# Batch 4's q through the DMA crossbar as well, with a new order and three fewer filler matmuls

## The chip, the cores and the metric

The kernel runs on one core of a Trainium2 chip, one launch, all inputs in HBM. The time is the device time of one execution in microseconds (us); less is better. TensorE (PE) multiplies matrices and writes PSUM, VectorE (DVE) and ScalarE (ACT) work element by element and read PSUM, GpSimd (POOL) here makes a few small products and issues most loads, and SyncE (SP) issues DMA transfers. Each engine runs its instructions in the order in which they were issued.

## What is computed

An attention of the kind in which k and v are first multiplied, and then a gated channel mix on its output. Cut to what matters:

```python
# q, k, v: (8 batches, 8 heads, 576, 64)
q_s = softmax(q, axis=-1)              # over the 64 of a head
k_s = softmax(k, axis=2)               # over the 576 positions
kv  = einsum('bhsd,bhse->bhde', k_s, v)
x   = einsum('bhsd,bhde->bhse', q_s, kv)   # then heads side by side: (8, 576, 512)
x_prev = x shifted by one position
xk = mu_k * x + (1 - mu_k) * x_prev
xr = mu_r * x + (1 - mu_r) * x_prev
k  = relu(xk @ w_k)                    # 512 -> 1024
v  = (k * k) @ w_v                     # 1024 -> 512
out = sigmoid(xr @ w_r) * v
```

Inputs and output are float32; the products are made in bfloat16.

## The kernel before, in words

Batches are taken one after another, and of each batch two groups g of four heads: `b4g1` below is batch 4, group 1, and an operation's name carries both (`scale41`, `B41`). A group's q, k and v arrive in three loads of 576 KB each (`load41q0`, `load41k0`, `load41v0`), issued by POOL into 11 buffers; batches 0 and 1 are cut finer.

For one group: ACT takes exp of q and k (`expq`, `expk`, L345) and casts v (`cast`, L352); DVE sums q's rows (`rsum`, L360), inverts the sums (`rrec`, L364) and scales (`scale`, L369). The scaled q must be turned, so that the 64 of a head lie on partitions. This is done in one of two ways:

- For batches 2 to 4 TensorE turns it: 36 (or, in larger pieces, 18) transposes into PSUM (L386), and one ACT copy of PSUM into the buffer `qt` (`qt40`, L397).
- For the batches in `CROSS` the DMA turns it: one `dma_start_transpose` on SP's queue from `qs` to `qt` (`tq50`, L559), from SBUF to SBUF.

k and v are multiplied on TensorE (L419). DVE makes weights of the product (`rz`, `w`, L426 and L436). The product of the turned q with these weights (L576) is `x`. From batch 2 on the pieces are joined into blocks on TensorE: block `B41` first makes `x` of the group before it (b4g0), then turns its own q if TensorE does that, and then multiplies its own k and v. So `B41` waits for q of b4g0 to be turned. Behind it ACT copies `x` (`xb`, `xs`) and DVE makes the two mixes (`edge`, `diff`, `sc`, `mix`, L589 to L603). Batches 0 and 1 have smaller steps for the same work: `Z` (sums of k, L406), `KV`, `T` (turning q, L386), `rz`, `kvn`, `qt`, `wp` (weights, L509) and `X` (L520).

The channel mix runs over 4608 positions in 11 units of 256 to 512 columns: `k5_3` is unit 5, piece 3 of the 8 of w_k (L680), followed by `relu` on ACT (L659) and `sq` on DVE (L669). For each of 36 tiles of 128 positions there are `r17` (L713), `th17` (tanh on ACT, L718), `v17_0` and `v17_1` (L733), `o17` (DVE, L739) and two stores `st17` (L749) on SP's queue.

What sets the order is the string `ORDER`: one list of all operations of all engines by name. Each engine executes its own in the order of the list; PSUM banks and buffers stand behind the colon. `POOL!` before a name chooses an engine. `^name` behind a name is a hold: the operation also waits until the named one is done, for a load until it has landed.

```python
name, _, held = name.partition("^")
...
if op.held:
    tc.add_manual_dep(op.made.ins, op.held.made.ins.name, sync)
```

At the start, before data is there, TensorE multiplies zeros: 19 `fill` (512 columns, L302) and `GAPS` small ones, `fillgap` (256 columns, L311), whose places are in the list too. Their output is not used.

Of the kernel before, what the change touches and what calls it, by code (L numbers as in the profile page):

```python
# [56 lines left out]
X0000:0 edge01 wp010:1 ACT!x0001b load11k0:6 x0000a DVE!x0010 X0100:1 ACT!x0000b X0101:3 x0100a  # L57
X0011:0 ACT!x0101b load11v1:7 x0100b k0_0:0 x0101a k1_0:1 x0011 k0_0.2 POOL!wp011 k1_0.2 k1_3:2
relu1_0:0 k1_7:3 load11k1 k0_1 k0_2:1 relu0_0:1 X0110:1 k1_3.2 load10q1 sq0_0 k1_7.2 k1_5:0
relu1_7:2 k0_2.2 load11v0 expq111:2 X0111:0 sq1_7 DVE!x0110 k0_4:3 wv0 relu1_3:1 k1_5.2 k0_4.2  # L60
sq1_0 relu1_5:2 k1_4:2 load10v0:8 rsum111:2 k0_5 expq110 k1_6:0 k1_4.2 sq1_3 relu0_4:0 k1_6.2
sq1_5 rrec111 relu1_4:1 x0111 k0_6:3 k0_3 relu1_6:2 k1_1:2 expq100:1 sq0_4 k1_2:0 k0_6.2 rsum110
relu0_2:0 wv1 k1_2.2 k1_1.2 k0_7 sq0_2 load10v1 r1:1 rrec110 relu1_1:0 scale110:2 load10k0:9 r2:2
sq1_1 scale111 load10k1 relu1_2:0 th1:0 r0:0 cast111:0 expk111:2 wv2 sq1_6 rsum100:3 T11:1 expq101
cast110 r3:1 expk110 sq1_2 load20q0:10 rsum101 relu0_6:2 KV11 th0:1 rrec101 sq1_4 th3:2 rz11:2
kvn11:0 load20v0:0 v0_0:3 sq0_6 th2:3 DVE!wp111:0 ACT!cast100:1 load21q0:1 v1_0:0 qt111:2 rrec100
qt110 scale101:0 v3_0:1 load30q0:2 scale100 v1_1 wp110 cast101 v0_1 load20k0:3 expk100:0 T10:0
v3_1 DVE!qt100:1 expk101 qt101 X1101:1 KV10 edge10 ACT!x1101 edge11 rz10:0 v0_2 kvn10:1 v3_2
POOL!wp100:1 o0 v1_2 load21v0:4 X1001:1 expq200:0 o1 X1000:0 X1110:3 load21k0:5 x1001 st1 v2_0:0
x1000 load30k0:7 DVE!x1110 cast200:2 X1111:1 load31q0:6 rsum200:1 X1100:0 k2_1:2 load40q0:8 x1100  # L70
v2_1 k2_7:3 expq210:2 wp101 rrec200 o3 k2_1.2 v2_2 load61v0:9 relu2_1:0 k2_2:1 o2 k2_7.2 expq300:1
load50k0:10 k2_0:2 x1111 k2_2.2 relu2_7:1 sq2_1 k2_5:0 rsum300:0 load31k0:0 k2_0.2 expk200:1
k2_4:3 X1010:0 relu2_2:2 X1011:1 scale200:1 load40v0:1 k2_4.2 relu2_0:0 k2_3:1 x1010 k2_6:2 sq2_7
cast210:0 k2_3.2 sq2_0 load30v0:2 k2_5.2 x1011 k2_6.2 relu2_5:1 rsum210:2 TKV20:0 relu2_4:0
load40k0:3 expk210:2 r5:0 rz20:1 rrec300 rrec210 r7:3 w20:0 th5:4 sq2_5 load31v0:4 scale210:2
relu2_3:1 r6:0 qt20:0 r4:1 load41q0:5 scale300:0 th7:5 B21:1.0 expq310:0 sq2_2 sq2_4 r8:3 rz21:2
relu2_6:2 sq2_3 load41v0:6 rsum310:3 xs20:0 th4:6 v4_0:2 xb20 v6_0:1 sq2_6 w21:1 th6:7 rrec310
edge20 v4_1 diff20:0 qt21:2 v6_1 scale310:1 th8:8 X21:0.1 v5_0:0 xb21:1 sc2001:0 sc2000 v4_2 o6
xs21 expk300:0 v7_0:3 edge21 st6 mix200 v5_1 st0 cast300:1 diff21:1 load51q0:7 st3 v7_1 sc2101:1
st2.2 expk400:1 sc2100 load60q0:2 mix210 st0.2 TKV30:0 cast310:2 o7 st3.2 load41k0:3 k3_4:1 st2 o5  # L80
expq400:2 k3_0:3 load70v0:4 sc2011:2 rz30:0 sc2111:0 k3_6:0 w30:2 relu3_4:0 sc2110 load70q0:8
sc2010 relu3_0:1 o4 k3_1:1 expk310:2 mix201 k3_5:3 mix211 relu3_1:2 load61q0:0 k3_3:2 qt30:1 sq3_1
sq3_4 k3_2:1 sq3_0 relu3_3:2 rsum400:1 relu3_5:0 B31:1.0 relu3_2:1 rrec400 k3_7:2 sq3_3 xb30:0
sq3_2 sq3_5 v8_0:3 xs30 relu3_6:2 rz31:1 scale400:2 r9:1 relu3_7:1 expq410:1 v10_0:0 sq3_7 w31:0
edge30 th9:9 sq3_6 r10:2 load50q0:5 diff30:1 cast400:0 v9_0:1 sc3001:1 sc3000 qt31:0 load51v0:1
sc3011:2 v8_1 mix300 expk500:0 B40:0.1 rsum410:2 th10:1 v10_1 load71v0:10 rz40:2 o8 xb31:1 r11:2
o10 st8.2 xs31 expq700:0 st5 edge31 v11_0:3 diff31:0 st6.2 v9_1 th11:2 sc3100:0 load71q0:8 st5.2
sc3101 expq510:2 rrec410 st7 v11_1 sc3010 mix310 st4 expk410:2 r12:0 load61k0:7 scale410:0 st8
k4_6:2 th12:3 load70k0:3 o11 expq500:1 k5_6:0 o9 k4_7:3 rsum510:0 relu4_6:0 st9.2 load51k0:5
k4_3:1 relu4_7:1 st10 cast510:1 k5_4:2 st9 rrec510 sq4_7 k4_0:3 sc3110:1 relu4_3:2 sc3111  # L90
load50v0:1 sq4_6 k5_5 relu4_0:1 mix311 k5_2:1 relu5_4:0 k5_7 sq4_0 cast410:2 k4_2:3 sq5_4 w40:1
scale510:1 k4_5:2 relu4_2:1 load71k0:6 relu5_6:0 k4_1:3 mix301 expq600:2 sq4_3 k5_3 sq4_2 k4_4:0
relu4_1:2 sq5_6 load60k0:2 rsum500:3 relu4_5:1 k5_0:3 relu4_4:0 r14:2 qt40:2 rsum600:1 k5_1 r13:0
th14:7 sq4_1 cast500:0 rrec600 B41:1.0 rrec500 sq4_5 sq4_4 th13:4 load60v0:1 scale600:2 v13_0:2
xs40:1 relu5_0:2 r15:0 xb40 rz41:0 sq5_0 w41:2 v12_0:3 relu5_2:1 edge40 diff40:1 th15:8 v15_0:1
qt41:1 scale500:0 v13_1 expk510:1 sc4001:0 tq50:0 B50:0.1 o13 st10.2 cast600:2 v12_1 rsum700:2
v15_1 xb41:0 rz50:1 o12 r16:0 expk610:2 w50:0 st12 sq5_2 v14_0:2 sc4010:1 st13.2 sc4000 xs41 o15
expk710:0 st13 v16_0:3 edge41 st12.2 mix400 th16:9 r17:1 st7.2 sc4011 expq710:2 diff41:0 tq51:2
B51:1.0 sc4110:2 cast610:0 v16_1 rrec700 sc4101:0 sc4100 v17_0:0 mix410 expk600:1 rz51:2 o16 v14_1
th17:1 mix401 expq610:1 k6_4:3 o14 k6_0:1 v17_1 sc4111 xs50:1 st14 xb50 w51:1 mix411 st4.2 k6_1  # L100
k6_2:2 rsum610:0 st1.2 relu6_0:0 B60:1.0 st11.2 k6_3 tq60:1 xb51:0 sq6_0 k6_5 st15.2 rz60:0
rrec610 edge50 r19:1 o17 st11 relu6_4:2 diff50:1 xs51 st16 k6_6:0 th19:4 r18:3 edge51 diff51:0
expk700:1 k6_7 sc5101:0 r20:1 sc5000:1 th18:3 sc5100 relu6_2:1 sq6_4 r21:3 w60:2 relu6_6:0 sq6_2
sq6_6 v19_0:2 th21:5 sc5010:2 mix510 th20:6 v18_0:0 sc5001 mix500 v19_1 sc5011 B61:0.1 o19 k7_3:3
sc5110:0 mix501 k7_2:1 scale700:0 relu7_3:2 xb60:1 k7_0:2 scale610:1 relu7_2:1 k7_6:3 relu7_0:0
k7_1:1 sc5111 tq61:0 rz61:1 sq7_3 tq70:2 mix511 v18_1 relu7_6:2 st14.2 cast700:1 sq7_6 k7_4:2
sq7_2 rsum710:1 relu7_1:2 k7_5:3 relu7_4:1 r23:1 o18 sq7_1 k7_7:2 sq7_0 th23:0 w61:0 relu7_5:2
r25:0 xs60 relu7_7:0 edge60 sq7_4 B70:1.0 sq7_7 rrec710 v21_0:1 diff60:1 xs61:0 xb61 v22_0:3
sc6000:1 th25:2 edge61 diff61:0 v20_0:2 cast710:2 sc6001 r22:0 rz70:2 sc6110:2 sq7_5 w70:1 v21_1
# [12 lines left out]
th31:3 st27.2 o31 v30_0:0 relu10_6:2 relu10_5:0 st31.2 k10_1:2 st28 sq10_5 v30_1 st28.2 relu10_1:0
st22.2 sq10_1 r34:3 sq10_6 sq10_7 st31 v32_0:1 o30 th34:5 st17.2 r32:2 st30 st23 v32_1 th32:4
v35_0:3 o32 v33_0:0 st32.2 v34_0:2 st30.2 st32 r33:1 v33_1 th33:9 v34_1 o33 r35:1 st33.2 o34 st33
v35_1 th35:2 st34 v35_0.2:0 st34.2 o35 v35_1.2 st35.2 st35 o35.2 st35.4 st35.3
"""


# [770 lines left out]
```

## Time and profile before

| | us |
|---|---|
| median of 3 runs | 198.97 |
| lowest, highest | 198.77, 198.99 |
| the profiled execution's own time | 198.85 |
| its span, from the first to the last instruction | 196.9 |
| TensorE busy in the span | 188.0 (95%) |
| VectorE busy | 151.9 (77%) |
| ScalarE busy | 134.9 (69%) |
| GpSimd busy | 47.7 (24%) |

HBM is read for 33.56 MB and written for 9.44 MB; the mean granted TensorE clock is 0.98. The profile's page gives totals over the span; its views by stretch, by time and by engine, and the chain of work that ended last, give single instructions with their start and length in us. A matmul's length in these views includes its way through the array, so the time that it takes in a row of matmuls is read from one start to the next.

### The profile page before, as it was taken

The page shows a single profiled execution, that of the slowest core. Times are in us where ns is not written, and L with a number is a line of the kernel's source. Part 1 is how long each engine was busy: PE and PEld are TensorE (multiplying, and loading weights), DVE is VectorE, ACT ScalarE, POOL GpSimd, SP SyncE. Part 2 cuts the span into 40 slices and gives each one's busy share as a digit, 9 for nine tenths or more (in the row PEclk, how much of TensorE's full clock was granted, in tenths as well). Part 3 has the DMA queues.
Part 4 walks back from the last instruction along what each step waited for, and adds up shares of the span by engine and source line. Part 5 has one row for each costly group of instructions (what it writes and reads, how often), then busy time and mean ns, then how long its engine had stood idle before and what let it go on. Part 6 is the DMA issues. An engine that isn't in the chain of part 4 may idle for free.

```text
span 196.9 us, 4779 instructions
## 1 busy us (share of the span) xinstructions
PE 188.0 (95%) x1894; PEld 96.1 (49%) x1916; DVE 151.9 (77%) x343; ACT 134.9 (69%) x213; POOL 47.7 (24%) x79
## 2 busy tenths in 40 slices
...
GB/s 188 348 203 295 348 256 359 398 239 392 392 389 387 315 416 297 298 312 413 318 148 168 103 171 64 16 134 0 57 168 107 0 42 41 19 142 118 202 83 160
DMA packets 23702, 41.87 MB, mean 213 GB/s; under 512 B 9460, under 2 KB 12800, under 8 KB 23680
## 3 DMA queue, kind: packets, MB, share of 16 engines
...
q14 instruction: 7, 0.06, 0.1%
HBM read 33.56 MB, written 9.44 MB: 218 GB/s over the span
## 4 chain that ended last, share of the span: by engine, by line
PE 79%; DVE 9%; ACT 5%; DMA 2%; issue 2%; POOL 0%; DVEq 0%; POOLq 0%
PE mm_b L680 9%; PE mm_c L680 8%; PE mm_d L680 8%; PE mm_d L733 7%; PE mm_c L733 7%; PE mm_a L733 7%; PE mm_a L680 6%; PE mm_a L713 4%; PE mm_b L733 4%; PE mm_b L713 4%; PE mm_c L713 2%; DMA raw_a<-in_q_dram 2%; PE mm_d L713 2%; PE att_a L419 2%; PE att_b L419 1%
## 5 line engine op out<-in xcount | busy, mean ns | idle before, releaser
L733 PEld LDWEIGHTS <-k 128*128 128x128 bf16 x296 | 28.0, 98 | 31.4 <-issue 0.5
L713 PEld LDWEIGHTS <-xr 128*128 128x128 bf16 x144 | 13.8, 98 | 15.8 <-issue 0.8
L669 DVE TENSOR_TENSOR k<-rel_b 128x512 bf16<-128x512 bf16 (+2 forms) x24 | 10.2, 427 | 6.5 <-ACT rel_b L659 6.4
L669 DVE TENSOR_TENSOR k<-rel_a 128x512 bf16<-128x512 bf16 (+2 forms) x27 | 11.1, 412 | 4.2 <-ACT rel_a L659 4.0
L669 DVE TENSOR_TENSOR k<-rel_c 128x512 bf16<-128x512 bf16 (+2 forms) x25 | 10.1, 402 | 4.3 <-ACT rel_c L659 4.1
L713 PE MATMUL mm_a<-wr,xr 128*128 128x512 bf16 x47 | 12.3, 379 | 0.6 <-ACT rel_a L659 0.5
L713 PE MATMUL mm_b<-wr,xr 128*128 128x512 bf16 x46 | 12.2, 379 | 0.2
L680 PEld LDWEIGHTS <-wk_ba 128*128 128x128 bf16 x88 | 8.3, 98 | 7.8 <-issue 0.5
L680 PEld LDWEIGHTS <-wk_ab 128*128 128x128 bf16 x88 | 8.5, 98 | 7.1 <-issue 0.2
L680 PEld LDWEIGHTS <-wk_bb 128*128 128x128 bf16 x88 | 8.5, 98 | 7.1 <-issue 0.2
L680 PEld LDWEIGHTS <-wk_aa 128*128 128x128 bf16 x88 | 8.3, 98 | 7.5 <-issue 0.5
L733 PE MATMUL mm_d<-wv_a,k 128*128 128x512 bf16 (+1 forms) x43 | 10.8, 369 | 0.1
L733 PE MATMUL mm_a<-wv_a,k 128*128 128x512 bf16 (+1 forms) x39 | 9.8, 369 | 0.1
L733 PE MATMUL mm_c<-wv_a,k 128*128 128x512 bf16 x35 | 9.2, 379 | 0.1
L659 ACT ACTIVATE rel_c<-mm_d 128x512 bf16<-128x512 f32 (+1 forms) x9 | 5.2, 580 | 5.1 <-issue 3.2
L680 PE MATMUL mm_b<-xk,wk_ab 128*128 128x512 bf16 (+3 forms) x34 | 8.6, 334 | 0.0
L680 PE MATMUL mm_b<-xk,wk_aa 128*128 128x512 bf16 (+3 forms) x34 | 8.6, 334 | 0.0
L659 ACT ACTIVATE rel_c<-mm_b 128x512 bf16<-128x512 f32 (+1 forms) x8 | 4.8, 595 | 4.8 <-PE mm_b L680 4.0
L680 PE MATMUL mm_d<-xk,wk_bb 128*128 128x256 bf16 (+3 forms) x30 | 7.4, 328 | 0.0
L680 PE MATMUL mm_d<-xk,wk_ba 128*128 128x256 bf16 (+3 forms) x30 | 7.4, 328 | 0.0
L733 PE MATMUL mm_b<-wv_a,k 128*128 128x512 bf16 x27 | 7.0, 379 | 0.2 <-issue 0.2
L680 PE MATMUL mm_c<-xk,wk_bb 128*128 128x512 bf16 (+3 forms) x24 | 6.5, 352 | 0.1
...
## 6 DMA issues: line engine op xcount, KB each, us to landing
raw_d<-in_k_dram POOLq DMA_DIRECT2D x4, 576.0 KB, 8.9
raw_b<-in_v_dram POOLq DMA_DIRECT2D x4, 576.0 KB, 6.6
raw_e<-in_v_dram POOLq DMA_DIRECT2D x3, 576.0 KB, 9.2
raw_i<-in_q_dram POOLq DMA_DIRECT2D x3, 576.0 KB, 8.5
...
raw_c<-in_q_dram POOLq DMA_DIRECT2D x2, 576.0 KB, 8.3
raw_f<-in_k_dram POOLq DMA_DIRECT2D x2, 576.0 KB, 7.2
```

The source lines that it names most:

```text
L419: kn.nc.tensor.matmul(kn.half(slot, r)[two[u], KVO:KVO + n], lhsT=kn.eks[ek.index][two[r], j, u, :], rhs=by, start=(j == 0), stop=(j == J ...
L659: kn.nc.scalar.activation(out=kn.rels[rel.index][:, 0:width], in_=kn.bank(kf)[:, 0:width], func=ACT.Relu, scale=HALF_ROOT)
L669: kn.nc.vector.tensor_tensor(out=to, in0=src, in1=src, op=ALU.mult)
L680: kn.nc.tensor.matmul(kn.bank(kf)[:, lo:lo + n], lhsT=kn.wk[fc // 4][ct % 2][:, ct // 2, (fc % 4) * 128: (fc % 4) * 128 + 128], rhs=kn.xs[ ...
L713: kn.nc.tensor.matmul(kn.bank(rps), lhsT=kn.xs[1][:, ct, c:c + 128], rhs=kn.wr[:, ct, :], start=(ct == 0), stop=(ct == CT - 1))
L733: kn.nc.tensor.matmul(kn.bank(vps)[:, 0:width], lhsT=kn.k2[:, ft, at:at + 128], rhs=wv_of(ft)[:, part], start=(ft == 0), stop=(ft == FT - 1))
```

## The change

Batch 4 joins `CROSS`: both its groups' q are turned by the DMA, `tq40` and `tq41`, and the transposes on TensorE in `B40` and `B41` and the ACT copies `qt40` and `qt41` are gone. `GAPS` falls from 14 to 11: three `fillgap` are gone, and the eleven left all stand ahead of `T01`, the first transposes. The whole list from the first q on is written anew.

In the new list, holds keep loads and transposes apart: `tq40`, `tq41` and `tq50` wait until `load60q0` has landed; the last five loads stand behind `load71q0`, which waits until `tq50` is done; `tq51` and `tq60` wait until `load71k0`, the last load, has landed.

```diff
-GAPS = 14
+GAPS = 11
-CROSS = (5, 6, 7)
+CROSS = (4, 5, 6, 7)
 ORDER = """
...
-rrec010 expk000 fillgap:2 fillgap.2:3 fillgap.3:2 rrec011 scale010:0 wk11 Z00:0 scale011
-fillgap.4:2 fillgap.5:3 fillgap.6:2 fillgap.7:3 fillgap.8:2 expk010:1 load11q1:4 scale001:1 T01:1
-load10q0:5 expk011 fillgap.9:2 fillgap.10:3 fillgap.11:2 rz00:0 widecopy mucopy scale000 KV001
-ACT!qt011:0 KV000 rest T00 qt010 fillgap.12:2 fillgap.13:3 kvn00:0 DVE!qt000:1 Z01 POOL!wp000:0
-fillgap.14:2 qt001 KV011 wp001 KV010 load11q0 X0001:3 edge00 rz01:1 X0010:2 wr kvn01:1 x0001a
+wk10 mu:1 expk001 fillgap:2 fillgap.2:3 fillgap.3:2 fillgap.4:3 scale010:0 wk11 Z00:0 fillgap.5:2
+fillgap.6:3 fillgap.7:2 fillgap.8:3 fillgap.9:2 fillgap.10:3 fillgap.11:2 rrec011 expk011:1
+load11q0:4 scale011 widecopy rz00:0 scale001:1 T01:1 KV000 scale000 ACT!qt011:0 KV001 expk010
+DVE!qt010 T00 rest mucopy kvn00:0 KV010 qt001:1 POOL!wp001:0 DVE!qt000 Z01 KV011 edge00 load10q0:5
+wp000 X0010:3 rz01:1 load11q1 X0001:2 kvn01:1 edge01 x0010 wp010:1 load10q1 X0000:0 wp011 x0001a
...
+cast510:1 v9_0:3 rsum500:3 v11_1 th11:1 load60q0:10 k4_5:2 o8 rz40:2 rrec410 k4_6:1 sc3111:0
...
+relu4_6:2 cast410:2 st2 k4_3:2 sq4_2 sq4_5 o9 tq40^load60q0:1 k5_4:1 relu4_3:1 k5_1 scale410:1
+expq600:1 k4_0:3 sq4_6 k5_5 tq41^load60q0:2 relu4_0:0 rsum510:2 k5_6:2 relu5_4:2 k4_1:3 expk410:2
+tq50^load60q0:0 w40:1 k4_4:1 sq4_0 sq5_4 relu5_0:0 mix301 k5_7 st11 cast500:0 B41:1.0 mix311 st4.2
...
+r16:3 st3 xb40 sq5_6 k5_2:1 w41:2 relu4_7:2 edge40 load71q0^tq50:6 rrec600 B50:0.1 sq4_4 expk510:1
+sq4_1 load61q0:10 k5_3 diff40:1 v12_0:0 relu5_2:1 load61v0:2 sq4_7 th16:3 sc4000:2 v13_0:1
+load71v0:7 sc4010:1 xs41:1 sc4011 load71k0:0 scale510:2 th13:1 v15_0:3 xb41 v12_1 sc4001 cast600:2
...
+B51:1.0 th15:5 r14:0 expk700:0 sc4101:0 sc4100 r17:2 o15 mix410 st15.2 v17_0:3 th17:6 o13 th14:0
+k6_0:2 tq51^load71k0:1 rz51:2 expq710:2 v17_1 w51:1 mix401 k6_1 o17 xs50:0 xb50 k6_4:1 sc4111:2
...
+diff50:1 cast710:0 st12 k6_2:2 mix411 st13.2 relu6_4:2 B60:1.0 o16 st3.2 k6_3 xb51:1 rz60:0
+sc5001:0 tq60^load71k0:2 k6_7 sc5000 sq6_0 r20:1 relu6_6:1 mix500 xs51 v14_0:0 relu6_2:0 sq6_6
...
 """
```

The parts left out reorder the same operations as in the list before.

More of the change, by code (lines that the diff above doesn't have):

```diff
@@ L56 @@
-fillgap.14:2 qt001 KV011 wp001 KV010 load11q0 X0001:3 edge00 rz01:1 X0010:2 wr kvn01:1 x0001a
[L57 to L109, printed above, removed]
@@ L122 @@
[L122 to L125, printed above, removed]
+load01v expq010:1 wk00 expq011 rrec001 rrec000 rsum010:1 wide:0 wk01 expk000:0 rrec010 rsum011
+wk10 mu:1 expk001 fillgap:2 fillgap.2:3 fillgap.3:2 fillgap.4:3 scale010:0 wk11 Z00:0 fillgap.5:2
@@ new lines @@
+load11k0 k1_0:1 relu1_3:1 sq1_7 k0_5 expq110:2 k0_0:3 load11v0 k1_0.2 k0_0.2 relu0_4:2 rsum110:2
+k1_4:0 relu1_0:0 k1_5:2 sq1_3 expq111 k1_2:1 sq0_4 k1_5.2 sq1_0 k1_2.2 rsum111 relu1_5:1 k1_4.2
+cast111:0 k0_1 relu1_2:2 k0_6:2 sq1_5 wv0 relu1_4:0 k1_6:1 rrec110 expq101:1 sq1_2 k0_2:0
+scale110:2 load10k1:9 k0_6.2 relu0_0:1 X0111:1 load10v0 rrec111 k0_7 expq100 rsum101:3 k1_6.2
+k1_1:3 relu0_6:2 load10k0 k0_2.2 rrec101 k1_1.2 sq0_0 ACT!x0111 k0_3 rsum100 wv1 r0:2 relu1_1:1
+sq0_6 expk111:2 wv2 r1:3 sq1_4 rrec100 th0:0 load20q0:10 scale100:0 relu1_6:2 r2:2 th1:1
@@ new lines @@
+load21q0:0 sq1_6 scale111 ACT!cast110 r3:1 sq1_1 relu0_2:0 scale101 T11:0 expk110 T10:1
+ACT!cast101:1 KV11 qt101:2 load20v0:1 v3_0:3 qt110:1 sq0_2 th3:2 qt111 v0_0:0 rz11:2 expk101:0
+cast100 kvn11:0 DVE!qt100 v1_0:1 edge11 expk100 wp110:0 edge10 DVE!wp111 X1100:0 KV10 x1100 v0_1
+rz10:0 kvn10:1 X1111:0 POOL!wp100:1 X1101:1 x1111 v1_1 ACT!x1101 load31q0:2 X1001:0 th2:3 X1000:1
+load20k0:3 ACT!x1001 v0_2 DVE!x1000 v3_1 load21v0:4 expq200:0 o0 v1_2 load21k0:5 k2_7:2 k2_3:0
+rsum200:1 expq210:2 wp101 k2_7.2 v3_2 load30q0:6 relu2_7:2 o1 X1011:0 X1110:1 cast200:2 load30k0:7
```

60 lines of the change are left out of this document (47 added, 13 removed).

## The prediction

> **What bounds the kernel now.** I read the page's busy times first, then the busy times by stretch, the chain of work that ended last, TensorE's timeline around the blocks of batches 4 and 5, and the transfers.
>
> The page's first line gives the totals; the view by stretch, with borders that I put at the first `X`, at `TKV20`, at `B51` and at the last matmul, gives busy time of TensorE, its weight loads, VectorE, ScalarE and GpSimd, then the granted clock:
>
> ```profile
> PE 188.0 (95%) x1894; PEld 96.1 (49%) x1916; DVE 151.9 (77%) x343; ACT 134.9 (69%) x213; POOL 47.7 (24%) x79
> ...
> 11.20:18.00 6.80, 6.80 (x164) 5.17 (x162) 4.15 (x15) 2.89 (x8) 4.04 (x9) 0.51 1.21 250
> 15.25:50.05 34.80, 33.57 (x394) 19.02 (x390) 28.84 (x66) 26.84 (x49) 23.64 (x39) 0.96 1.05 330
> 50.05:107.55 57.50, 56.87 (x721) 28.97 (x729) 55.59 (x115) 55.92 (x79) 14.45 (x20) 1.00 0.94 322
> 107.55:138.00 30.45, 30.03 (x353) 15.93 (x359) 28.52 (x67) 21.93 (x35) 0.00 (x0) 1.00 0.40 84
> 193.20:196.90 3.70, 0.02 (x1) 0.00 (x0) 0.42 (x1) 0.00 (x0) 0.00 (x0) 0.83 0.50 150
> ```
>
> From 50 us on TensorE is busy for all but 1 us in 88, so this part is as long as TensorE's list. The third row also shows VectorE and ScalarE idle for only 1.9 and 1.6 us of 57.5: three engines are nearly full there. Ahead of it lies a stretch at half clock (0.51), and behind it a tail of 3.7 us, a last gating and a store.
>
> The chain, in order of time, shows the steady rate and the tail (start, us, what):
>
> ```profile
> 46.36 0.38 PE mm_c L680 x2
> ...
> 189.32 0.86 PE mm_a L733 x4
> ...
> 193.25 0.42 DVE th_c L739
> ```
>
> Four matmuls of 512 columns take 0.86, one `r` or half a `v`; half a `k` piece of unit 2 takes 0.38. The tail has the same steps in both lists (a half `o35` and its stores behind the last matmul) and is taken at nothing. The span of 196.9 lies in an execution of 198.85; the sum is made against that, and the median of the runs, 198.97, stands 0.12 above it.
>
> **The transposes that go.** TensorE's timeline around `B40` and `B41`:
>
> ```profile
> 78.03 0.48 PE L386 MATMUL att_a<-ident,qs_c 64*64 64x64 bf16 x36
> 78.32 0.49 PE L419 MATMUL att_a<-vv_a,ek_b 64*64 64x65 bf16 x36
> ...
> 96.42 0.48 PE L386 MATMUL att_b<-ident,qs_a 64*64 64x64 bf16 x36
> 96.72 0.49 PE L419 MATMUL att_b<-vv_c,ek_c 64*64 64x65 bf16 x36
> ```
>
> From the first transpose to the product that follows it is 0.29 and 0.30 us. Both go: 0.59, taken as 0.6, all on the path, since TensorE waits for nothing around them. Bounds: 0, if something else is late there, and 0.96 if their whole lengths of 0.48 counted.
>
> The two ACT copies go too:
>
> ```profile
> 94.15 1.11 ACT L397 COPY qt_c<-att_a 128x1152 bf16<-128x1152 bf16 x1
> 100.05 1.17 ACT L397 COPY qt_b<-att_b 128x1152 bf16<-128x1152 bf16 x1
> ```
>
> That is 2.3 us less for ScalarE. It is off the path, since TensorE does not wait in that stretch; I take nothing for it.
>
> **The transposes that come.** Two on SP's queue, and holds between them and the loads. The nearest rows are the transposes of batches 5 to 7 (SP's issue, then issue to landing), the last load, and two lengths to landing of loads between 60 and 100 us:
>
> ```profile
> 101.42 1.40 SPq L559 DMA_TRANSPOSE qt_a<-qs_a  x1
> ...
> qt_a<-qs_a SPq DMA_TRANSPOSE x1, 4.6
> qt_b<-qs_c SPq DMA_TRANSPOSE x2, 3.2
> ...
> 97.46 0.72 POOL L212 DMA_DIRECT2D raw_b<-in_v_dram  x1 [3.67 <-ACT vv_a L352]
> ...
> raw_f<-in_q_dram POOLq DMA_DIRECT2D x1, 576.0 KB, 4.4
> raw_f<-in_k_dram POOLq DMA_DIRECT2D x1, 576.0 KB, 8.3
> ```
>
> `tq40` is wanted by `B41`. In the new list, between the place of `load60q0` and `B41`, TensorE has seven `k4` and one half `v9` at 0.86 and six `k5` of half the columns: 9.5 us, and up to 0.9 more of the half `v11` at whose side the load stands, so 10.4. The load and the transpose take 4.4 + 3.2 = 7.6 to 8.3 + 4.6 = 12.9 us. So this costs between nothing and 2.5 us. I take nothing: only three loads stand close ahead of this one, which is nearer to the late loads with 4.4 than to the crowd with 8.3. The cover is thin, some 1.4 us with a 4.6 us transpose.
>
> Behind `tq40` on SP wait `tq41`, `tq50` and stores. `tq41` is wanted one block later, with 6.5 us of TensorE work between its place and `B50`; the stores free buffers of which ten are in turn. On POOL, four loads wait behind `load71q0` until `tq50` is done. From the place of the last of them, `load71k0`, to `B60`, which needs `tq51` behind it, TensorE has 13.0 us (12 pieces at 0.86, five at half of it, and a block); 8.3 + 4.6 = 12.9 just fits. Without that cover every us late is a us lost. Taken at nothing.
>
> **The start.** The chain there, and the timeline of the other engines on the way to the first `X`:
>
> ```profile
> 10.47 0.11 PE mm_d L311
> ...
> 11.53 0.21 PE mm_d L311
> ...
> 13.46 0.33 PE mm_c L311
> 13.79 0.21 PE mm_d L311
> ...
> 14.34 0.33 PE mm_c L311
> ```
>
> ```profile
> 10.52 0.15 DVE L295 COPY mu<-mm_b 128x8 f32<-128x8 f32 x1
> ...
> 10.58 0.75 DVE L369 TENSOR_TENSOR qs_b<-eq_a,rrec_a 128x576 bf16<-128x576 bf16 x1
> ...
> 11.69 0.42 DVE L286 TENSOR_SCALAR mu_wide<-mu_wide 128x512 f32<-128x512 f32 x1
> ...
> 13.51 0.29 DVE L436 TENSOR_TENSOR kvn_a<-att_a,rz_a 128x128 f32<-128x128 f32 x1 [1.40 <-PE att_a L386]
> 13.84 0.64 ACT L395 COPY qt_b<-att_a 128x576 bf16<-128x576 bf16 x1 [1.39 <-DVE kvn_a L436]
> 13.96 0.87 POOL L509 TENSOR_TENSOR wp_a<-kvn_a,mu_wide 128x128 bf16<-128x128 f32 x2 [2.95 <-DVE kvn_a L436]
> 14.51 0.46 DVE L395 COPY qt_b<-att_a 128x576 bf16<-128x576 bf16 x1 [0.70 <-ACT qt_b L395]
> ...
> 15.25 0.44 PE L520 MATMUL mm_c<-qt_b,wp_a 64*64 64x288 bf16 x1
> 15.28 0.19 DVE L503 COPY qt_b<-qt_b 128x126 bf16<-128x126 bf16 x1
> ```
>
> A `fillgap` costs 0.11 before 11.2 us and 0.21 behind it: the clock has halved. The last three stand between `T00` and the first `X` and take 0.33 + 0.21 + 0.33 = 0.87 of the chain. They are the ones that the new list has no longer there. Behind them the second q of b0 waits on VectorE: with `rz00` now ahead, the two scalings end about 0.75 later than before, at 12.15. From there by the rows: one copy of q 0.46, the wide mu 0.42, the small mu 0.15, so `kvn00` from 13.15 to 13.45; the DVE copy 0.46 to 13.9; the ACT copy, which now follows it, 0.64 to 14.55; the edge 0.19 to 14.75. POOL's weights (0.87 from about 13.5) are done at 14.4. TensorE's products, without the fillers, end near 14.3. So `X0010` starts at about 14.8 where the first `X` started at 15.25: 0.45 earlier. Bounds: nothing, if one of these steps slips, and 0.87, all three fillers.
>
> The stretch from there to `TKV20` is reordered as a whole. TensorE idles for 1.23 of its 34.8 us, so there is at most that to win. Against it, `T10` now stands directly behind `T11` and wants two more scalings ahead of it; but by `X1101` both lists have the same TensorE work behind them within 0.2 us, and the new one 0.7 of VectorE more. Taken at nothing, between 1.2 won and 0.7 lost.
>
> **VectorE's share.** Four rows for its costs:
>
> ```profile
> 45.11 0.75 DVE L532 CAST xr<-att_b 128x576 bf16<-128x576 f32 x1
> 54.48 0.38 DVE L669 TENSOR_TENSOR k<-rel_c 128x448 bf16<-128x448 bf16 x1
> 102.29 1.35 DVE L360 TENSOR_REDUCE rsum_c<-eq_a 128x18 f32<-128x1152 bf16 x1
> 103.63 0.67 DVE L739 SCALAR_TENSOR_TENSOR th_d<-th_d,mm_d 128x512 f32<-128x512 f32 x1
> ```
>
> Between `TKV20` and `B51` the new list gives TensorE four short groups more at the front (two halves of `k2` at 0.38 and two quarters of `v` at 0.43: 1.62) and takes four of 0.86 (`r14`, `r17`, `v14_0`, `v16_0`: 3.45) away behind `B51`; with the 0.6 of transposes, 2.4 us less. VectorE gets as much as it loses: at the front one sum, one `o`, one copy and on balance no `sq` (1.35 + 0.67 + 0.75 = 2.77), at the back a sum and two `o` (2.69). So its 55.6 us of work meet 55.1 of TensorE's. This costs between nothing and 2.4 (the idle 1.9 kept). I take nothing: `mix410`, the VectorE step of this stretch that the first `k6` piece wants, has `B51`, `r14`, `r17` and `v17_0` ahead of that piece on TensorE, 3.5 us of cover for a VectorE that runs late, and later VectorE has room (1.9 idle of 30.45). Without the cover it is the first rival.
>
> **Sum.** 198.85 − 0.6 − 0.45 = 197.80, and with 0.12 up to the median 197.9.
>
> **Rivals.**
> - VectorE becomes the bound between 50 and 108 us. For it: 55.59 busy of 57.5 already, and the same work for 2.4 us less of TensorE. Against it: the 3.5 us of cover. It loses up to 2.4: 197.9 + 2.4 = 200.3 at worst, 199.4 at 1.5. It turns the sign from 1.05 us of waiting on.
> - `load60q0` lands late, and `B41` waits for `tq40`. It decides from a landing 5.8 us behind its place (10.4 − 4.6); at 8.3 the loss is 2.5, 200.4; at 7.3 it is 1.5, 199.4. For it: the row with 8.3, and stores that share the engines. Against it: only three loads stand within 5 us ahead of it, and none behind it until `tq50` is done.
> - The clock. It halved at 11.2 and came back near 18, 6.8 us or, as I estimate, two stretches of 3.4 later; it is granted by what TensorE did in a stretch. With less work at 14.3 to 14.8 it could stay low for one stretch more: TensorE then does 1.7 of 3.4 us of work, 197.9 + 1.7 = 199.6. With more fillers ahead of `T01` it could instead come back, or not fall, one stretch earlier: 196.2. The Trainium skill ("TensorE: Matmul & The Clock Gate", Part 1) says that the gate judges free-running windows of about 3.4 us, which do not start with the kernel. By that rule either is possible; that the two changes lie about two such windows apart agrees with it.
> - The start gains nothing, and only the transposes count: 198.85 + 0.12 − 0.6 = 198.4.
>
> **How the numbers follow.** About 0.2%, 0.4 us, is what a measurement can tell from no change. Chances: the forecast 0.42, its own range 197.3 to 198.6; the start without gain 0.12; VectorE as the bound 0.20; the late load 0.13; the clock low for longer 0.06; high for longer 0.07. Faster than 198.57: nearly all of the forecast (0.39), most of the start without gain (0.08) and the high clock (0.07): 0.54. Within 0.4 of before: what is left of these two and the mild ends of the two waits: 0.12. Slower: 0.34. Forecasts of both signs hold weight, so the range goes from 196.8 to 200.2: it leaves out the high clock and the worst ends of the two waits.
>
> **What would show it.** Right: no transposes of TensorE between 50 and 110 us, 0.9 us for `B40` and `B41` alike, `X0010` near 14.8, TensorE idle for no more than about 1 us from `TKV20` to 138 us, and `tq40` landed before `B41`. Wrong: a wait of `B41` on a transpose, idle TensorE released by VectorE's `mix`, `sq` or `w` between 50 and 125 us, a first `X` at 15.2 or later, or half-rate matmuls behind 18 us.

## The result and the profile after

| | before | after |
|---|---|---|
| median of 7 runs each, us | 198.79 | 196.9 |
| lowest, highest | 198.59, 198.99 | 196.42, 197.98 |
| the profiled execution's own time | 198.85 | 196.49 |
| its span | 196.9 | 194.7 |

The ratio is 0.9909 (0.9886 to 0.9931): 1.9 us less, where 1.05 was forecast. A ratio, here and below, compares only runs within 1.5% of the quickest of their kernel. The runs of after lie 1.6 us apart, those of before 0.4; the profiled execution of after is one of its quick ones, 0.41 below its median.

The page's first line of after, and the view by stretch with borders at its first `X`, `TKV20`, `B51` and the start of the last matmul group (span, then busy time of TensorE, its weight loads, VectorE, ScalarE and GpSimd, granted clock, DMA share, GB/s):

```profile
PE 184.9 (95%) x1819; PEld 93.9 (48%) x1841; DVE 148.4 (76%) x343; ACT 133.7 (69%) x214; POOL 46.4 (24%) x76
...
11.20:18.00 6.80, 5.39 (x185) 3.80 (x177) 4.63 (x18) 4.10 (x11) 4.32 (x8) 1.00 1.20 253
13.88:45.90 32.02, 30.59 (x378) 17.15 (x374) 25.23 (x64) 27.55 (x52) 22.00 (x35) 1.00 1.09 331
45.90:101.02 55.12, 54.49 (x642) 27.60 (x649) 53.73 (x115) 51.43 (x74) 15.60 (x22) 1.00 0.98 341
...
189.76:194.70 4.94, 0.38 (x4) 0.10 (x1) 0.75 (x2) 0.23 (x1) 0.00 (x0) 0.80 0.50 133
```

The clock did not halve between 11 and 18 us here (1.00, before 0.51). From `TKV20` on TensorE idles as little as before (0.63 of 55). The tail is longer: 4.94 from the start of the last matmul group, where before had 196.9 − 192.84 = 4.06. Four marks of TensorE's timeline of after (the first `X`, the first `k` piece, `T11`, the last group):

```profile
13.88 0.28 PE L521 MATMUL mm_c<-qt_b,wp_a 64*64 64x288 bf16 x1
...
17.70 0.39 PE L681 MATMUL mm_c<-xk,wk_ba 128*128 128x256 bf16 x2
...
29.57 0.44 PE L387 MATMUL att_a<-ident,qs_c 64*128 64x64 bf16 x18
...
189.76 0.38 PE L734 MATMUL mm_c<-wv_c,k 128*128 128x256 bf16 x2
```

From these the 2.20 us between the spans are split as follows.

| | before | after | difference | of it list steps moved | won (−), lost (+) |
|---|---|---|---|---|---|
| to the first `X` | 15.25 | 13.88 | −1.37 | | −1.37 |
| first `X` to `TKV20` | 34.80 | 32.02 | −2.78 | −1.62 | −1.16 |
| `TKV20` to the last group | 142.79 | 143.86 | +1.07 | +1.62 | −0.55 |
| last group to the end | 4.06 | 4.94 | +0.88 | | +0.88 |

The 1.62 are the four short groups of the prediction, which now stand behind `TKV20`; they are the sum of its rows, not a length of their own in this trace. The first `X` is an early mark and not yet a gain: of its 1.37 us only 0.65 are left at the first `k` piece (18.35 before, 17.70 after). From there to `TKV20` the trace of before takes 31.70 us, or 30.08 without the 1.62, and that of after 28.20: here the larger part, 1.88, was won.

### The profile page after: what moved, and what is told of

The parts are those of the page before. It is cut to its first block, busy times and chain, and to the rows that moved or that the text cites. A ratio compares the mean times of both kernels' runs of the same rounds, so it can differ in the third digit from the quotient of the medians.

```text
span 194.7 us, 4639 instructions
## 1 busy us (share of the span) xinstructions
PE 184.9 (95%) x1819; PEld 93.9 (48%) x1841; DVE 148.4 (76%) x343; ACT 133.7 (69%) x214; POOL 46.4 (24%) x76
## 4 chain that ended last, share of the span: by engine, by line
PE 80%; DVE 7%; DMA 6%; issue 2%; ACT 1%; POOL 1%; ACTq 0%; DVEq 0%; POOLq 0%
PE mm_c L681 10%; PE mm_b L734 9%; PE mm_a L734 8%; PE mm_d L734 8%; PE mm_b L681 8%; PE mm_d L681 7%; PE mm_c L714 5%; PE mm_c L734 4%; PE mm_a L681 4%; PE mm_d L714 4%; PE mm_a L714 3%; DMA mu_rows<-in_moe_mu_r_dram 3%; DMA raw_c<-in_q_dram 3%; PE mm_b L714 3%; DVE k L670 1%
## 5 line engine op out<-in xcount | busy, mean ns | idle before, releaser
L660 ACT ACTIVATE rel_a<-mm_c 128x512 bf16<-128x512 f32 (+1 forms) x11 | 6.6, 599 | 9.7 <-PE mm_c L681 9.6
L714 PE MATMUL mm_c<-wr,xr 128*128 128x512 bf16 x47 | 12.3, 379 | 0.1
L734 PE MATMUL mm_b<-wv_a,k 128*128 128x512 bf16 x42 | 11.2, 379 | 0.1
L714 PE MATMUL mm_d<-wr,xr 128*128 128x512 bf16 x40 | 10.3, 379 | 0.0
L734 PE MATMUL mm_a<-wv_a,k 128*128 128x512 bf16 x38 | 10.2, 379 | 0.1
L681 PE MATMUL mm_c<-xk,wk_ba 128*128 128x512 bf16 (+3 forms) x34 | 8.6, 334 | 0.0
L660 ACT ACTIVATE rel_c<-mm_c 128x512 bf16<-128x512 f32 (+1 forms) x8 | 4.8, 595 | 4.5 <-PE mm_c L681 2.9
L681 PE MATMUL mm_c<-xk,wk_aa 128*128 128x512 bf16 (+2 forms) x28 | 7.4, 347 | 0.0
L681 PE MATMUL mm_c<-xk,wk_ab 128*128 128x512 bf16 (+2 forms) x26 | 7.0, 344 | 0.0
L660 ACT ACTIVATE rel_b<-mm_d 128x512 bf16<-128x512 f32 (+2 forms) x10 | 5.8, 577 | 1.5 <-PE mm_d L681 1.5
```

What stands on the lines that cost most here:

```text
L660: kn.nc.scalar.activation(out=kn.rels[rel.index][:, 0:width], in_=kn.bank(kf)[:, 0:width], func=ACT.Relu, scale=HALF_ROOT)
L681: kn.nc.tensor.matmul(kn.bank(kf)[:, lo:lo + n], lhsT=kn.wk[fc // 4][ct % 2][:, ct // 2, (fc % 4) * 128: (fc % 4) * 128 + 128], rhs=kn.xs[ ...
L714: kn.nc.tensor.matmul(kn.bank(rps), lhsT=kn.xs[1][:, ct, c:c + 128], rhs=kn.wr[:, ct, :], start=(ct == 0), stop=(ct == CT - 1))
L734: kn.nc.tensor.matmul(kn.bank(vps)[:, 0:width], lhsT=kn.k2[:, ft, at:at + 128], rhs=wv_of(ft)[:, part], start=(ft == 0), stop=(ft == FT - 1))
```

## The experiments

Each kernel ran beside runs of the kernel before on the same chip, whose medians were 198.69 to 198.94.

### The tail: e1_tail

```diff
-v35_1.2 st34.2 st34 v35_0:2 th35:1 st33.2 v35_1
+v35_1.2 st34 v35_0:2 th35:1 st34.2 st33.2 v35_1
```

> The new kernel with one store moved in the list: the second store of tile 34, which ScalarE issues, stands behind the last tanh instead of ahead of it. Nothing else. In the profile of the new kernel this store's issue holds the last tanh until 1.2 us behind the last r, and the tail from the last matmul to the end is 4.56 us against 3.68 before. If that store is what makes the tail longer: the tail is back at about 3.7 us, the time 0.85 us below the new kernel's, near 196.0. If the tail is set by the last gating and its stores anyway (rival): no change, 196.9.

Measured: 196.26 us (196.17 to 196.50), ratio 0.9869 (0.9852 to 0.9886). The timeline of after at the end:

```profile
188.72 0.55 ACTq L750 DMA_DIRECT2D out_dram<-th_d  x1
...
189.39 0.60 ACT L719 ACTIVATE th_b<-mm_a 128x512 f32<-128x512 f32 x1 [5.06 <-PE mm_d L734]
...
190.02 0.42 DVE L740 SCALAR_TENSOR_TENSOR th_b<-th_b,mm_d 128x256 f32<-128x256 f32 x1 [1.33 <-ACT th_b L719]
190.36 0.41 DVE L740 SCALAR_TENSOR_TENSOR th_b<-th_b,mm_c 128x256 f32<-128x256 f32 x1
```

and that of e1_tail:

```profile
189.02 0.60 ACT L719 ACTIVATE th_b<-mm_a 128x512 f32<-128x512 f32 x1 [4.53 <-PE mm_a L714]
189.08 0.54 ACTq L750 DMA_DIRECT2D out_dram<-th_d  x1
...
189.65 0.42 DVE L740 SCALAR_TENSOR_TENSOR th_b<-th_b,mm_d 128x256 f32<-128x256 f32 x1 [0.80 <-ACT th_b L719]
...
190.33 0.42 DVE L740 SCALAR_TENSOR_TENSOR th_b<-th_b,mm_c 128x256 f32<-128x256 f32 x1 [0.26 <-PE mm_c L734]
```

The stores of the last two tiles are issued in part by ScalarE. In after it issues one, which waits for VectorE's `o34` and takes 0.55, ahead of the tanh of the last tile. The first half of `o35` then waits for the tanh (190.02), the second stands behind it (190.36), and the last stores follow. With the store behind the tanh, the last step waits for TensorE alone (190.33, 0.26 behind it). The tail falls from 4.94 to 4.49 (189.91 to a span of 194.4); the rest of the 0.64 between the medians lies within the spread of after (196.42 to 197.98). The 0.43 by which 4.49 is over the 4.06 of before is taken up below.

### The clock and the small fills: e3_before_fills, e4_after_fills

e3 is the old kernel with the eleven fills where the new list has them; e4 is the new kernel with fourteen where the old list had them. The cut shows the edit of e3, from the first fill on; that of e4 is its reverse in the new list.

```diff
-GAPS = 14
+GAPS = 11
-fillgap:2 fillgap.2:3 fillgap.3:2 rrec011 scale010:0 wk11 Z00:0 scale011
-fillgap.4:2 fillgap.5:3 fillgap.6:2 fillgap.7:3 fillgap.8:2 expk010:1 load11q1:4 scale001:1 T01:1
-load10q0:5 expk011 fillgap.9:2 fillgap.10:3 fillgap.11:2 rz00:0 widecopy mucopy scale000 KV001
+fillgap:2 fillgap.2:3 fillgap.3:2 fillgap.4:3 rrec011 scale010:0 wk11 Z00:0 scale011
+fillgap.5:2 fillgap.6:3 fillgap.7:2 fillgap.8:3 fillgap.9:2 fillgap.10:3 fillgap.11:2 expk010:1
+load11q1:4 scale001:1 T01:1 load10q0:5 expk011 rz00:0 widecopy mucopy scale000 KV001
...
-qt010 fillgap.12:2 fillgap.13:3 kvn00:0 DVE!qt000:1 Z01 POOL!wp000:0
-fillgap.14:2 qt001
+qt010 kvn00:0 DVE!qt000:1 Z01 POOL!wp000:0 qt001
```

> The kernel before with the filler layout of the new one: four small fillers ahead of Z00, seven between Z00 and T01, none behind; everything else as before. Theory of the clock: what the start won (2.5 us in the profiles: the first X 1.4 earlier, the work up to TKV20 1.2 shorter) came from a clock that no longer halves at 11.2 us, because the fillers stand densely ahead of that time; then here the clock stays up too, the mean granted clock is 0.99 or more, the first X starts near 14, and the time falls by 1.5 to 2.5 us to 196.3 to 197.3. Theory of the order: the new list's shorter chain won it; then here the clock halves as before and only the three late fillers are saved, 0.3 to 0.9 us: 197.9 to 198.5.

> The new kernel with the filler layout of the one before: three small fillers ahead of Z00, five between Z00 and T01, three behind T01, two behind T00, one behind Z01; the rest of the new list stays. Theory of the clock: the clock halves near 11 us, the mean granted clock is 0.98, and the time is 1.5 to 2.5 us above the new kernel's, 198.4 to 199.4. Theory of the order: the fillers cost their own 0.3 to 0.9 us and no more: 197.2 to 197.8.

Measured: e3 198.66 us (198.49 to 199.13), ratio 0.9996 (0.9986 to 1.0006); e4 196.76 (196.50 to 197.50), ratio 0.9899 (0.9879 to 0.9919). The old list with the new fills gains nothing, although its clock was full and its first `X` came at 13.75; the new list with the old fills loses nothing. So the fills did not make the gain. Of the clock e4 says nothing, since it was 1.00 between 11.2 and 18 us in its profiled execution too; against the theory of the clock stand e3, with a full clock and no gain, and, in the new list, e1_tail, with a half clock and hardly a loss. The views by stretch of e1_tail and e3:

```profile
11.20:18.00 6.80, 6.80 (x182) 5.40 (x177) 4.54 (x18) 4.00 (x12) 4.37 (x9) 0.54 1.20 253
```

```profile
11.20:18.00 6.80, 5.10 (x177) 3.52 (x176) 4.62 (x16) 3.77 (x10) 4.62 (x9) 1.00 1.21 253
24.00:30.00 6.00, 5.13 (x34) 3.12 (x33) 5.74 (x12) 3.42 (x9) 5.10 (x9) 1.00 1.16 282
```

e1_tail ran this stretch at half clock (0.54) with a busy TensorE, and had `TKV20` at 46.06, 0.16 behind after with its full clock and its idle 1.4 us. A second trace of the new list at half clock, that of e6 below (0.53), has it at 46.03; the five others with the same list up to there (clock 0.75 to 1.00) lie between 45.76 and 46.28, so a half clock there costs next to nothing. e3, at full clock, idles instead: 1.7 us in the first stretch, 0.87 in the second, where VectorE is busy for 5.74 of 6. It has its first `k` piece 0.45 us ahead of before, and `T11` at 30.52, where before had 30.53. What ate the 0.45 stands in VectorE's and GpSimd's timeline, of before:

```profile
26.19 0.68 POOL L352 CAST vv_a<-raw_h 128x576 bf16<-128x576 f32 x1
26.54 0.62 DVE L669 TENSOR_TENSOR k<-rel_a 128x512 bf16<-128x512 bf16 x1 [0.22 <-ACT rel_a L659]
...
27.32 1.50 DVE L369 TENSOR_TENSOR qs_c<-eq_c,rrec_c 128x576 bf16<-128x576 bf16 x1
27.52 0.68 POOL L352 CAST vv_a<-raw_h 128x576 bf16<-128x576 f32 x1
```

and of e3:

```profile
26.09 1.05 DVE L668 TENSOR_TENSOR k<-rel_a 128x512 bf16<-128x512 bf16 x1 [0.22 <-ACT rel_a L658]
26.17 0.68 POOL L351 CAST vv_a<-raw_h 128x576 bf16<-128x576 f32 x1
...
27.30 1.50 DVE L368 TENSOR_TENSOR qs_c<-eq_c,rrec_c 128x576 bf16<-128x576 bf16 x1
...
28.96 0.75 DVE L368 TENSOR_TENSOR qs_c<-eq_c,rrec_c 128x576 bf16<-128x576 bf16 x1
```

The same scaling takes 0.75 alone and 1.50 beside GpSimd's cast. The product `k` starts 0.45 us earlier in e3 and ends at the same 27.15, 0.3 us behind the cast's end (26.85). Behind it wait ScalarE's next relu and, through it, the `r` ahead of `T11`, which TensorE starts after a wait of 0.81 us (0.50 in before).

### The casts: e7_old_cast, e8_old_cast_fills, e11_pool_casts

The old list has three casts of v of batch 1 on GpSimd and one on ScalarE; the new list has two of the four on ScalarE. e7 moves two in the old kernel to ScalarE, e8 is e3 with the same edit, and e11 moves the new kernel's two back to GpSimd.

```diff
-r0:0 cast111:0 expk111:2
+r0:0 ACT!cast111:0 expk111:2
...
-expq101 cast110 r3:1
+expq101 ACT!cast110 r3:1
```

```diff
-ACT!cast110 r3:1
+cast110 r3:1
...
-ACT!cast101:1 KV11
+cast101:1 KV11
```

> The old kernel with two casts of v of batch 1 (cast111, cast110) on ScalarE in the place of GpSimd, where they run from 26.19 and 27.52 us; nothing else changed. Theory of the casts: VectorE's product k at 26.54 (0.62 in the place of 0.42) and its scaling at 27.32 (1.50 in the place of 0.75) are stretched only while GpSimd casts; without that VectorE is 0.95 us ahead, the r group ahead of T11 does not wait 0.5 us for its relu, and the kernel takes 198.0 to 198.4 us. Theory of the order alone: the stretch makes no difference, T11 comes at 30.5 and TKV20 at 50.0 us as before, 198.8 us within 0.2.

> e7_old_cast with the new kernel's places for the small fills as well, as in e3_before_fills, which had full clock and a first k piece 0.45 us earlier and was no faster. Theory of the casts: there the gain at the start was lost because VectorE's product k started at 26.09 in the place of 26.54 and ended at the same 27.15, when GpSimd's cast was done; with the casts away the 0.45 is kept: 197.6 to 198.0 us. Theory that something else absorbs the start (loads, the order): the same as e7_old_cast within 0.15.

> The new kernel with the two casts of v of batch 1 that it has on ScalarE (cast110 at 28.44, cast101 at 30.07 us) back on GpSimd. Theory of the casts: VectorE's scalings and products between 28 and 31 us are stretched by up to 0.7 each as in the old kernel, T10 or the steps behind it wait, 197.3 to 198.0 us. Rival, in the new list VectorE has 1 to 2 us of room between 24 and 36 us (8.9 busy of 12), so a stretch is absorbed: 196.9 within 0.25.

Measured: e7 198.33 us (198.01 to 199.38), ratio 0.9985 (0.9971 to 0.9998); e8 198.00 (197.66 to 198.19), ratio 0.9959 (0.9946 to 0.9971); e11 197.75 (197.53 to 198.12), ratio 0.9939 (0.9925 to 0.9953). The timeline of e8:

```profile
25.75 0.42 DVE L668 TENSOR_TENSOR k<-rel_a 128x512 bf16<-128x512 bf16 x1 [0.22 <-ACT rel_a L658]
...
26.33 0.76 DVE L368 TENSOR_TENSOR qs_c<-eq_c,rrec_c 128x576 bf16<-128x576 bf16 x1
...
29.08 0.44 PE L385 MATMUL att_b<-ident,qs_c 64*128 64x64 bf16 x18
```

No step is stretched between 25.4 and 31.4 us, and `T11` comes 1.45 us before that of before, `TKV20` 0.85 (49.20). With the casts away, the same fills that gave e3 nothing are worth 0.33 (e8 against e7; the intervals of the ratios touch) and the edit of the casts 0.66 (e8 against e3; they lie apart). In e7 alone `T11` came 0.74 earlier (29.79), but `KV11` then waited 0.71 for ScalarE's exponential, which stands behind the casts there, as it does in e8: the gain of 0.44 is hardly more than its interval. The reverse, in e11's timeline:

```profile
17.49 0.39 PE L681 MATMUL mm_c<-xk,wk_ba 128*128 128x256 bf16 x2
...
28.11 0.71 POOL L353 CAST vv_a<-raw_g 128x576 bf16<-128x576 f32 x1
28.22 1.21 DVE L370 TENSOR_TENSOR qs_c<-eq_c,rrec_c 128x576 bf16<-128x576 bf16 x1
28.77 1.18 POOL L353 CAST vv_b<-raw_i 128x576 bf16<-128x576 f32 x1
29.35 0.78 DVE L670 TENSOR_TENSOR k<-rel_b 128x320 bf16<-128x320 bf16 x1
...
30.86 0.44 PE L387 MATMUL att_b<-ident,qs_a 64*128 64x64 bf16 x18 [0.93 <-DVE qs_a L370]
...
46.76 0.44 PE L387 MATMUL att_a<-ident,qs_b 64*128 64x64 bf16 x18
```

A scaling is stretched from 0.75 to 1.21, a product from 0.32 to 0.78, `T10` waits 0.93 us, and `TKV20` comes at 46.76 in the place of 45.90. From the first `k` piece (17.49) to there e11 takes 29.27 us, where after and the eight other traces of lists that have these two casts on ScalarE (e1, e2, e4, e5, e6, e9, e10, e12) take 28.20 or 28.21: the casts cost 1.06 us there. At the end it is less sure: the medians are 0.85 apart, the ratios 0.003, or 0.6 us, and the intervals of the ratios overlap a little.

### The crossbar for batch 4: e2_pe_turn, e6_pe_turn2, e9_pe_turn3

All three are the new kernel with `CROSS = (5, 6, 7)`; they differ in where the ScalarE copies (and in e6 and e9 the first scaling of batch 4) stand; VectorE's `w40` and `w41` are moved forward with them.

```diff
-CROSS = (4, 5, 6, 7)
+CROSS = (5, 6, 7)
...
 e2: rrec410 w40:1 qt40:1 k4_6:1   ...   rz41:0 w41:2 qt41:2 sq5_0
 e6: sq3_3 rrec400 scale400:2 sq3_7   ...   rsum510:2 qt40:1 k5_6:2   ...   qt41:1 rrec600 B50:0.1
 e9: as e6 for scale400   ...   relu4_5:0 qt40:1 rrec500   ...   relu4_1:0 qt41:2 sq4_3
```

> The new kernel with q of batch 4 turned on TensorE again: 72 transposes back in B40 and B41, two ScalarE copies back, tq40 and tq41 gone; the rest of the list and the holds of the others stay. If the crossbar part is worth what its transposes took on TensorE: 0.55 to 0.6 us slower than the new kernel. If taking the two copies from ScalarE mattered too: 1 us slower or more, with TensorE idle ahead of B41 or B50. If it is hidden: no change.

> The new kernel with q of batch 4 turned on TensorE again, as in e2_pe_turn, but with the first scaling of batch 4 (rrec400, scale400) moved ahead of relu3_6, the ScalarE copy qt40 moved back behind rsum510 and the copy qt41 to just ahead of B50. Theory of the waits: of the 1.7 us by which e2_pe_turn is over the new kernel only 0.6 are the transposes, the rest are waits that came from where its ScalarE copies and its scaling stood (T40 0.3 for the scaling, a relu 0.5 behind a ScalarE that waits for VectorE's w41): 197.5 to 197.9 us. Theory of a full ScalarE: the two copies of 2.3 us cost over a us wherever they stand in this list: 198.4 us or more.

> The new kernel with q of batch 4 turned on TensorE again, as in e2_pe_turn, but with scale400 ahead of relu3_6 (as in e6_pe_turn2), the ScalarE copy qt40 behind relu4_5, where ScalarE waits for TensorE, and the copy qt41 behind relu4_1. Theory of the waits (e2_pe_turn lost 0.6 to transposes and 1.5 to waits, e6_pe_turn2 0.6 and 2.2, the latter 1.7 of it at B50 for the copy qt41): with both copies in gaps 197.5 to 197.9 us. Theory of a full ScalarE: over 198.4 again, with other waits in the place of these.

Measured: e2 198.61 us (198.14 to 198.95), ratio 0.9984 (0.9972 to 0.9996); e6 199.59 (199.38 to 200.10), 1.0043 (1.0029 to 1.0056); e9 198.46 (198.08 to 199.41), 0.9978 (0.9965 to 0.9990). By the medians, turning on TensorE again costs 1.6 to 2.7 us over after, not the 0.6 of its transposes. The rest are waits. In e2's timeline:

```profile
72.90 0.48 PE L387 MATMUL att_a<-ident,qs_c 64*64 64x64 bf16 x36 [0.30 <-DVE qs_c L370]
...
93.03 1.12 ACT L398 COPY qt_c<-att_b 128x1152 bf16<-128x1152 bf16 x1 [0.50 <-DVE w_c L437]
...
94.70 1.02 PE L714 MATMUL mm_d<-wr,xr 128*128 128x512 bf16 x4 [0.49 <-ACT rel_a L660]
```

The first row is the scaling, which the new list has just ahead of `B40`, early enough for a DMA that follows but not for transposes. The copy of the second row waits with all of ScalarE's queue behind it, and the third row pays. e6 cured the first, and paid elsewhere, in its chief wait of TensorE (total us, times, longest):

```profile
PE att_a L577 <- ACT qt_b L398: 1.7, 1, 1.7
```

e9 has both copies in gaps of ScalarE:

```profile
94.80 0.38 PE L681 MATMUL mm_b<-xk,wk_aa 128*128 128x256 bf16 x2 [0.56 <-ACT rel_b L660]
...
95.70 0.22 PE L577 MATMUL att_a<-qt_c,w_c 64*64 64x64 bf16 x4 [0.31 <-ACT xb_a L582]
```

Its `B51` comes at 103.01, 1.99 us behind that of after: 0.59 of transposes and 1.4 of waits, most of them behind the copy `qt41` between `B41` and `B50`, where ScalarE has no room. Of the two theories in the expectations, that of a full ScalarE is the nearer one, for the three places tried by hand; a list searched anew for it was not tried.

### The holds: e5_no_holds

```diff
-tq40^load60q0:1   tq41^load60q0:2   tq50^load60q0:0   load71q0^tq50:6   tq51^load71k0:1   tq60^load71k0:2
+tq40:1   tq41:2   tq50:0   load71q0:6   tq51:1   tq60:2
```

> The new kernel without the six waits between loads and transposes (tq40, tq41 and tq50 behind load60q0, load71q0 behind tq50, tq51 and tq60 behind load71k0); list and engines as in the new kernel. Theory A, the places in the list already keep loads and transposes apart and nothing near them is late: 196.9 us within 0.4, the transposes land 3 to 5 us behind their issue as now. Theory B, the holds carry part of the gain: the transposes run beside loads, land 8 us or more behind their issue, B41 or B50 waits for them, 198 us or more.

Measured: 206.92 us (201.57 to 208.69), ratio 1.0157 (1.0135 to 1.0179). The ratio stands on its two quickest runs, 201.57 and 202.21; the other four took 206.9 to 208.7. The profiled execution is the quickest, 201.57. Its transfers (the last figure is us from issue to landing), two issues on SP, and `B41`:

```profile
qt_b<-qs_c SPq DMA_TRANSPOSE x1, 8.1
qt_c<-qs_b SPq DMA_TRANSPOSE x1, 6.7
qt_a<-qs_a SPq DMA_TRANSPOSE x1, 13.4
...
raw_c<-in_v_dram POOLq DMA_DIRECT2D x1, 576.0 KB, 10.8
...
84.38 1.60 SPq L560 DMA_TRANSPOSE qt_b<-qs_c  x1
...
88.32 4.06 SPq L560 DMA_TRANSPOSE qt_a<-qs_a  x1
...
92.52 0.27 PE L577 MATMUL att_b<-qt_b,w_b 64*64 64x64 bf16 x4 [2.29 <-DMA qt_b<-qs_c]
```

The same three in after, with `tq40`'s issue and `B41`:

```profile
qt_b<-qs_c SPq DMA_TRANSPOSE x1, 3.4
qt_c<-qs_b SPq DMA_TRANSPOSE x1, 3.4
qt_a<-qs_a SPq DMA_TRANSPOSE x1, 3.3
...
85.79 1.35 SPq L560 DMA_TRANSPOSE qt_b<-qs_c  x1
...
89.93 0.22 PE L577 MATMUL att_b<-qt_b,w_b 64*64 64x64 bf16 x4
90.20 0.48 PE L420 MATMUL att_b<-vv_c,ek_c 64*64 64x65 bf16 x36
```

Without holds `tq40` was issued 1.4 us sooner and landed 3.3 us later, and `B41` waited 2.29 us. Behind that wait the granted clock was 0.55 from 93 to 96 us, and the way from `B41` to `B50` took 5.26 us in the place of 3.82. The holds cost nothing that the trace shows and, by the two quickest runs, save about 5 us (201.57 and 202.21 against 196.9). What the four longer runs waited for was not profiled, and no run took the six holds apart.

### A better end, and the spread: e10_tail2, e12_swap

```diff
-r35:0 st33 o34 v35_1.2 st34.2 st34 v35_0:2 th35:1 st33.2 v35_1
+r35:0 st33 st33.2 o34 v35_1.2 st34 v35_0:2 th35:1 st34.2 v35_1
```

e12 has besides:

```diff
-expq600:1 k4_0:3
+expk410:2 k4_0:3
...
-k4_1:3 expk410:2
+k4_1:3 expq600:1
```

> e1_tail (second store of tile 34 behind th35) with, besides, the second store of tile 33 on SP's queue directly behind the first, so that SP is done with it 0.6 us sooner, ahead of the last four stores. From the last matmul's start to the end before had 4.06 us, the new kernel 4.94, e1_tail 4.49. Theory that the left 0.43 is SP's queue: 195.8 to 196.1 us. Theory that it is the transfers themselves (the same bytes on the same engines): 196.26 within 0.15, as e1_tail.

> e10_tail2 with the two ScalarE exponentials expq600 and expk410 changing places, so that the one that waits for load60q0 runs 2.2 us later. In the slowest run of e10_tail2 (197.16 us, profiled) load60q0 took 7.6 us to landing in the place of 6.3; expq600 waited 1.09 us for it and TensorE 0.82 us for the relu behind it. Theory that this wait makes the spread of the new kernel's runs (196.4 to 198.0): all runs within 0.4 us of each other, median 196.0 to 196.2. Rival, the spread comes from elsewhere or the load is as late against its new place: median 196.3 and single runs near 197 as in e10_tail2.

Measured: e10 196.35 us (196.04 to 197.16), ratio 0.9876 (0.9857 to 0.9896); e12 196.37 (195.87 to 198.03), ratio 0.9895 (0.9866 to 0.9924). The tails took 4.36 and 4.39, so 0.1 of the 0.43 was SP's queue, and the theory of the queue falls for the most part. In both, the last half `o35` starts 0.42 behind the last group, 0.41 in before, so the other 0.3 lie behind it, at the last stores; why is open. At the median neither is better than e1_tail. The slowest run of e10 was the profiled one, and shows one cause of the spread (load, ScalarE, TensorE):

```profile
raw_k<-in_q_dram POOLq DMA_DIRECT2D x1, 576.0 KB, 7.6
...
87.17 1.16 ACT L346 ACTIVATE eq_b<-raw_k 128x1152 bf16<-128x1152 f32 x1 [1.09 <-DMA raw_k<-in_q_dram]
...
88.86 0.59 PE L681 MATMUL mm_d<-xk,wk_aa 128*128 128x512 bf16 x2 [0.82 <-ACT rel_a L660]
```

In after this load took 6.3 and nothing waited. But e12, which runs this exponential 2.2 us later, spreads as widely (195.87 to 198.03). Its profiled run, the quickest, has none of these waits; what its longest run waits for is open. A part of the spread is there from the start: in nine traces with the same list up to the first `k` piece, that piece starts between 17.49 and 18.07 us.

## Why the prediction was right, and which terms were off

The sign held, and the range just so: 196.9 lies 0.1 above its lower end of 196.8. The size did not: 1.05 forecast, 1.9 measured, and the likeliest case had a range of its own, 197.3 to 198.6, which the time misses. Of the two terms that the sum puts above nothing, the transposes came out as reckoned and the start did not. Three terms were mis-sized, two of them to one side (the start and the stretch, 2.1 us more won than forecast) and one to the other (the tail, 0.9 lost), so that the range held is in part luck.

- **The transposes, 0.6.** Right to the hundredth in the trace: the products of `B40` and `B41` follow each other by 0.22 (90.20 − 89.98 in `B41`), where before it was 0.51 and 0.52, and the stretch behind `TKV20` is 0.55 shorter.
- **The two ScalarE copies, taken at nothing.** Right for the old list, where TensorE did not wait. In the new list, with the copies back at three places tried by hand, 1.0 to 2.1 us more than the transposes were lost (e2, e6, e9). "Off the path" was a statement on the old list's cover and does not move over to the new one.
- **`tq40` in time, taken at nothing.** Right: the load landed after 6.3, within the bounds of 4.4 and 8.3, the transpose after 3.4, and 0.7 us were left at `B41` (85.79 + 3.4 = 89.2 against 89.93). These terms stand only with the holds: without them the transposes took 6.7 to 13.4. The rival of the late load did show itself, not at `B41` but at ScalarE's `expq600`, which the prediction had not followed.
- **The start, 0.45.** Its time came out within its bounds at the half clock that it was reckoned with: there the first `X` of the same list started at 14.60 (e1_tail, 0.54) and 14.49 (e6, 0.53), against 14.8. Its mark was wrong: the profiled execution of after had the full clock, and the first `X` came 1.37 earlier, outside the bounds of 0 to 0.87. That is of little worth: e4 has the old fills and loses nothing, and e1_tail lost 0.16 at `TKV20` by a half clock. The step that failed is to have counted time won at the first `X` as time won at the end, without asking what is late next.
- **The stretch to `TKV20`, taken at nothing between 1.2 won and 0.7 lost.** Here the gain was. Start and stretch together gave 1.37 + 1.16 = 2.53 where 0.45 was forecast. The trace of before had it in rows that were not read: a scaling of 1.50 beside ones of 0.75. The new list's `ACT!` ahead of two casts was taken for part of a reordering. The casts account for 1.06 of it in the new list (e11, from the first `k` piece to `TKV20`). The other 1.5 lie with the rest of the order, `T10` behind `T11` among it, by the marks of the traces alone; no run took that apart.
- **VectorE's share, taken at nothing.** Right: the stretch from `TKV20` to `B51` took 55.12 us, as forecast (57.5 − 2.4), TensorE idles for 0.63 of it, and the rival of a VectorE that becomes the bound did not come. It was nearly full earlier: from 24 to 36 us VectorE was busy for 11.3 us of 12 before, the stretched steps included, and for 8.9 after.
- **The tail, taken at nothing as "the same steps in both lists".** Wrong by 0.88, of which a store's place gave back 0.45 (e1_tail). The steps are the same; their order on ScalarE's queue is not: before, the stores of tile 34 stood behind the last tanh. Of the rest 0.1 was SP's queue (e10), and 0.3 stay open.
- **The clock as a rival.** It decided nothing. Some executions of before had a mean clock of 0.98 to 0.99 and some of 1.0, in the same time.
- **Two of the marks for "right" were ill drawn.** TensorE still turns batches 2 and 3 behind 50 us (transposes at 51.26, 58.61 and 66.67), and `B40` and `B41` take 0.69 us each, not 0.9.

The lowest median of all kernels run is that of e1_tail: 196.26 us, ratio 0.9869 (0.9852 to 0.9886).
